# Top-32 attention and an ELU feed-forward block: sign bit into the shifted word, first scores by head, weights ahead of a pair of keys

## The chip, the cores and the metric

The kernel runs on one core of a Trainium2 chip. The metric is device time in microseconds (us) of one execution, the median over several runs. The engines are named as the profile names them: PE multiplies matrices (PEld is its loading of weights), DVE is the vector engine, ACT the scalar engine, POOL is GpSimd, and SP issues most of the transfers. Each engine works through its own list of instructions in order, and waits on semaphores for what other engines or transfers produce.

## The reference

The first block is attention that keeps, for each query, only the keys whose score is at least the 32nd largest. Its output, with the heads laid side by side, goes through a feed-forward block with an ELU between two products.

```python
# q, k, v: (8, 8, 576, 64) float32
scores = (1 / sqrt(64)) * q @ k.T
kth = np.partition(scores, -32, axis=-1)[..., -32:-31]
scores = np.where(scores >= kth, scores, -1e9)
scores = scores - max(scores)
attn = exp(scores); attn = attn / (sum(attn) + 1e-9)
x = (attn @ v) with heads side by side            # (4608, 512)
h = x @ w_in                                       # w_in (512, 2048), float64
g = where(h > 0, h, exp(min(h, 0)) - 1)
out = (g @ w_out).astype(float32)                  # w_out (2048, 512), float64
```

The two weight matrices arrive as float64. The kernel sees them as pairs of 32-bit words and turns them into float32 itself.

## The kernel before

**Steps.** The attention is cut into steps. A step is one tile of 128 queries of one batch and a pair of heads (for the last 64 queries of a batch, two pairs). There are four steps for a full tile and two for the remainder. `steps` holds all of them in order, and the main loop runs over `n`, where it searches step n, exponentiates step n-1, and multiplies step n-1 or n-2 by v. The first six steps (`EARLY = 6`) have their own branch of the loop, which computes the scores two steps ahead.

**The search (DVE).** For each of the two heads of a step, the 32 largest of 576 scores are found in four rounds: `first_max` (MAX8 at L373) and three times `next_max`, which replaces the eight found by a very low number (MATCH_REPLACE8 at L379) and searches again (MAX8 at L387). The eighth of the last round is the 32nd largest score.

**The mask.** In the first six steps `mask_early` makes three small numbers from that score (DVE L413, POOL L416, L417, L420 and L394), ACT applies a Relu with them as scale and bias (L428), and POOL subtracts the result from the scores (L431), once for each head. Later steps use `mask` on POOL alone (L399 to L401). ACT then exponentiates (L439).

**Start.** `load_qk(b, hp)` loads keys and queries of a pair of heads; for the first two pairs of batch 0 the queries go through ACT's queue, all else through SP's. `transpose_qk` turns them on PE into `kq` (L299, L307; copies L291, L292, L294). `scores(u, half)` makes, for one half of the keys, the products of both heads (L348) and copies them to `sc` with one copy (L368): 576 columns, 288 of each head. So a search of either head needs both halves. For the very first step the first half is copied by ACT and the second by DVE. `warm(n)` issues n transposes of the identity matrix on PE whose result nobody reads (L318). PSUM has two buffers (`ps_x`) that the transposes and the scores share.

**Decoding the weights.** The weights are 32 blocks of 128 by 512. `load_weights(most)` takes up to `most` entries of the list `loads` and issues them on SP's queue (L172); the first entry is three blocks, the second one, the third three. `weight_slot()` is called at set places between the search's rounds through `decode(n, place)`; each call joins the block that was split two calls earlier and splits the next one. Splitting is two passes on ACT: L182 writes a float32 from the high word, scaled, to the weight's place `dst`, and L183 scales the low word in place. Joining is on DVE and POOL: L188 shifts the words of `dst` left by three bits, L189 puts the sign bit of the high word into a word, and POOL's L193 adds the low word to the shifted one. The steps 0 to 3 have four decode places each, steps 4 and 5 five.

**Feed-forward.** When all heads of a tile are done, `sums` inverts the denominators on DVE (L451, L452), they go through DRAM and come back broadcast (`rb`), POOL scales the tokens (L547, `normalise`), and the pieces of the feed-forward block (`hidden` L567, `project` L591, with L581 to L584 for the ELU) become ready. `feed` issues such pieces on PE between the attention's products.

Of the kernel before, what the change touches and what calls it, by code (L numbers as in the profile page):

```python
# [10 lines left out]
FP32 = mybir.dt.float32  # L11
# [50 lines left out]
def kernel(  # L62
# [9 lines left out]
    nc = tc.nc  # L72
    P = nc.NUM_PARTITIONS
    B, H, S, D = q.shape
    dm, dff = moe_w_in.shape[0], moe_w_in.shape[1] // 2
    J = S // P
    JP = J * P
    R = S - JP
    HS = S // 2
# [17 lines left out]
    scpool = pool("sc", 5)  # L97
# [8 lines left out]
    ps_x = pool("ps_x", 2, space=PSUM)  # L106
# [78 lines left out]
    def join_weight(i):  # L185
        low, high, dst = words(i)
        bits = dst.bitcast(U32)
        nc.vector.tensor_scalar(bits, bits, 3, None, ALU.logical_shift_left)  # L188
        nc.vector.scalar_tensor_tensor(  # L189
            out=low, in0=high, scalar=0x80000000, in1=low,  # L190
            op0=ALU.bitwise_and, op1=ALU.bitwise_or,
        )
        nc.gpsimd.tensor_tensor(bits, bits, low, ALU.add)  # L193
        decoded[0] += 1
        del raw[i]
# [17 lines left out]
    def load_qk(b, hp):  # L213

        first = b == 0 and hp < 2
        aside = (b, hp) in ((0, 1), (0, 2))
        if aside:
            home = xtpool.tile([P, 2, NC * T // 2], FP32, tag="xT", name="kqin")
            home = home[:, :, 0 : (J + 1) * 2 * D].rearrange(
                "p n (j h d) -> p n j h d", j=J + 1, h=2  # L220
            )
        for n, (name, src) in enumerate((("k", k), ("q", q))):
            queue = nc.scalar if first and name == "q" else nc.sync
            if aside:
                t = home[:, n]
            else:
                t = ldpool.tile([P, J + 1, 2, D], FP32, tag="in", name=name + "in")
            queue.dma_start(
                t[:, 0:J, :, :],
                src[b, 2 * hp : 2 * hp + 2, 0:JP, :].rearrange(  # L230
                    "h (p j) d -> p j h d", j=J
                ),
            )
            queue.dma_start(
                t[0:R, J, :, :],
                src[b, 2 * hp : 2 * hp + 2, JP:S, :].rearrange("h p d -> p h d"),
            )
            loaded[b, hp, name] = t
# [75 lines left out]
    def warm(n):  # L314

        ps = ps_o.tile([P, dm], FP32, tag="o", name="idle")
        for _ in range(n):
            nc.tensor.transpose(ps[:, 0:P], ident[:], ident[:])  # L318
# [12 lines left out]
    def scores(u, half, copy=nc.scalar.copy):  # L331
# [35 lines left out]
                product(i, u.hps[0], i, slice(0, P), 0, ks)  # L367
        copy(u.sc[:, :, ks], ps[:, :, 0:HS])  # L368

    def first_max(u):  # L370
        u.m1 = small.tile([P, 2, 8], FP32, tag="m1", name="m1", bufs=2)
        for i in range(2):
            nc.vector.max(u.m1[:, i, :], u.sc[:, i, :])  # L373
        u.wk = wkpool.tile([P, 2, S], FP32, tag="wk", name="wk")
        u.m, u.cur = u.m1, u.sc
# [13 lines left out]
    def biases(u, early):  # L389
        u.neg = small.tile([P, 2], FP32, tag="neg", name="neg", bufs=2)  # L390
        if not early:
            u.nth = small.tile([P, 2], FP32, tag="nth", name="nth", bufs=2)
            nc.gpsimd.tensor_scalar_mul(u.nth[:], u.m[:, :, 7], -1.0)
        nc.gpsimd.tensor_scalar_mul(u.neg[:], u.m1[:, :, 0], -scale)  # L394
# [5 lines left out]
        nc.gpsimd.tensor_scalar(pen, pen, 0.0, TAKEN, ALU.min, ALU.max)  # L400
        nc.gpsimd.tensor_tensor(s, s, pen, ALU.add)  # L401

    def mask_early(u, between=None):

        kth = u.m[:, :, 7]
        field = small.tile([P, 2], U32, tag="field", name="field", bufs=2)
        minus = small.tile([P, 2], FP32, tag="minus", name="minus", bufs=2)
        neg = small.tile([P, 2], FP32, tag="nth", name="nth", bufs=2)  # L410
        pos = small.tile([P, 2], FP32, tag="pos", name="pos", bufs=2)
        one = 2.0**23
        nc.vector.tensor_scalar(  # L413
            field[:], kth.bitcast(U32), 0x7F800000, None, ALU.bitwise_and
        )
        nc.gpsimd.tensor_scalar(minus[:], field[:], 67 * one, -1.0, ALU.max, ALU.mult)  # L416
        nc.gpsimd.tensor_scalar_add(neg[:].bitcast(U32), minus[:], 560 * one)  # L417
        for i in range(2):
            at = slice(i, i + 1)
            nc.gpsimd.tensor_scalar(  # L420
                pos[:, at], kth[:, at], neg[:, at], -1.0, ALU.mult, ALU.mult
            )
        biases(u, True)
        if between is not None:
            between()
        for i in range(2):
            pen, s = u.wk[:, i, :], u.sc[:, i, :]
            nc.scalar.activation(  # L428
                pen, s, AF.Relu, scale=neg[:, i : i + 1], bias=pos[:, i : i + 1]
            )  # L430
            nc.gpsimd.tensor_tensor(s, s, pen, ALU.subtract)  # L431
# [112 lines left out]
    def normalise(g):  # L544
        blk = g.block
        x = blk.xT[:, :, g.cols]
        nc.gpsimd.tensor_tensor(x, x, g.rb[:, :, 0 : g.ql], ALU.mult)  # L547
        blk.left -= 1
        if blk.left == 0:
            ffn.extend(ffn_pieces(blk))  # L550
# [97 lines left out]
    steps, first, order = [], {}, []  # L648
    for b in range(B):
# [4 lines left out]
        for qt in (0, 1, 2, 3, 4) if b % 2 == 0 else (4, 0, 1, 2, 3):  # L654
            r0 = b * S + (JP if qt == J else qt)
            if qt == J:
                if b % 2 == 0:
                    half = blk, slot = places.pop(0)
# [29 lines left out]
    def decode(n, place):  # L688

        if place in ((2, 3, 4, 5, 6) if n in (4, 5) else (3, 4, 5, 6)):  # L690
            weight_slot()
# [39 lines left out]
    with tc.manual_schedule():  # L731
        load_qk(0, 0)
        nc.scalar.activation(rec[:], rec[:], AF.Copy)
        for hp in (1, 2):
            load_qk(0, hp)
        load_weights(3)
        warm(16)
        for hp in range(2):
            transpose_qk(0, hp, shared=hp == 0)
            steps[hp].kq = {hp: kqT[0, hp]}  # L740
            scores(steps[hp], 0)
            scores(steps[hp], 1, nc.vector.tensor_copy if hp == 0 else nc.scalar.copy)
            if hp == 0:
                load_qk(0, 3)
        load_weights()
        load_v(0, 0)
        first_max(steps[0])
# [4 lines left out]
        for n in range(NS + 4):  # L752
# [39 lines left out]
            if early:  # L792
                decode(n, 0)
                feed(n, 0.5)
                if last:
                    exp(last, 0)
                    exp(last, 1)
                next_max(now, (n, 1))
                decode(n, 2)
                if last:  # L800
                    trans(last)
                feed(n, 0.5)
                next_max(now, (n, 3), last)
                decode(n, 4)
                if last:
                    attend(last)
                if n in turns:
                    transpose_qk(*turns[n])
                if n < EARLY - 1:
                    warm(24)  # L810
                next_max(now, (n, 5))
                tile_ends = last and last.ends
                mask_early(now, (lambda: normalise(last.g)) if tile_ends else None)
                decode(n, 6)
                if n >= NHP - 2:
                    load_next()
                continue
# [63 lines left out]
```

## Time and profile before

| what | value |
|---|---|
| median of 3 runs | 1624.78 us (1624.5 to 1625.08) |
| profiled execution | 1623.01 us, its span 1621.2 us |
| mean granted PE clock | 0.991 of full |
| L387 MAX8 | 864, 748 ns each, 609.8 us in all |
| L379 MATCH_REPLACE8 | 576 and 288, 743 and 744 ns each |
| L182, L183 split passes on ACT | 32 each, median 0.68 us |
| L188 shift on DVE | 32, median 0.42 us, first at 16.7, last at 124.6 us |
| L189 sign bit on DVE | 32, median 0.68 us, longest 1.88 us |
| L193 add on POOL | 32, median 1.29 us |
| first three raw weight blocks | issued by SP at 8.21, landed 15.21 us |

The span runs from the first to the last instruction of the profiled execution. A line of a timeline gives the start in us, the length in us, the engine, the line of the kernel, the operation, what it writes and reads, and in square brackets how long the engine had stood idle and what ended that. One instruction's recorded length can overlap the next one's start by some hundredths, since the engine takes up the next while the last results are on their way out; so the distance of starts is the better measure of what an instruction costs its engine. The share of busy time is an average over the whole span, and says nothing of a single stage. The first 40th of the span is about 40 us.

```profile
PE   7878999999999999999999999999999999999999
...
DVE  7999999999999999999999999989999999899700
```

These two lines give the busy tenths of PE and DVE in 40 slices of the span.

### The profile page before, as it was taken

Reading aid. Unit: us, or ns where it says so; the run is one execution under the profiler, and the core shown is the slowest. Engines: PE = TensorE matmul, PEld = TensorE weight load, DVE = VectorE, ACT = ScalarE, POOL = GpSimd, SP = SyncE. Lnnn points to the kernel's source line nnn. Section 1 sums busy time; section 2 is a strip of 40 time slices with the busy share of each in tenths; the row PEclk is TensorE's granted clock in tenths of the full one; section 3 lists DMA queues with packets and bytes.
Section 4 is the critical chain, followed back from the end, with each engine's and each line's share of the span. In section 5 each row is a group of like instructions: output and inputs, shape, how many; then the busy total and the mean of one; then the engine's idle time right before and its main releaser. Section 6 shows DMA issues by size and latency. Waiting matters only on the chain.

```text
span 1621.2 us, 28833 instructions
## 1 busy us (share of the span) xinstructions
PE 1560.3 (96%) x9948; PEld 1066.8 (66%) x9948; DVE 1474.9 (91%) x3070; ACT 905.5 (56%) x1857; POOL 1141.6 (70%) x1448
## 2 busy tenths in 40 slices
PE   7878999999999999999999999999999999999999
PEld 5765778777675858676565665565565585757665
DVE  7999999999999999999999999989999999899700
ACT  6875666555564756565574575465475364545321
POOL 3777777777786878778687687678677676767621
PEclk8989999999999999999999999999999999999999
DMA  9773454442121413232423524333332552453300
GB/s 311 246 219 120 147 180 141 131 129 104 42 111 51 152 58 117 72 94 82 119 71 104 183 80 116 108 102 103 109 113 76 151 161 96 121 135 89 87 13 14
DMA packets 226706, 188.70 MB, mean 116 GB/s; under 512 B 180480, under 2 KB 188672, under 8 KB 226560
## 3 DMA queue, kind: packets, MB, share of 16 engines
q1 hardware_dynamic: 224192, 186.26, 38.1%
q8 instruction: 79, 1.29, 0.3%
q10 hardware_dynamic: 2368, 0.59, 0.2%
q14 instruction: 67, 0.55, 0.1%
HBM read 151.26 MB, written 35.54 MB: 115 GB/s over the span
## 4 chain that ended last, share of the span: by engine, by line
PE 80%; DVE 8%; POOL 5%; ACT 3%; issue 2%; DMA 1%; SPq 0%; DVEq 0%; POOLq 0%; ACTq 0%
PE ops L591 27%; PE hps L567 27%; PE avps L532 9%; PE scps L348 9%; PE eps L481 6%; DVE m L387 3%; DVE wk L379 3%; POOL sc L401 1%; POOL gT L584 1%; POOL wk L399 1%; POOL wk L400 1%; PE eps L499 1%; DVE raw L189 1%; PE qkps L299 0%; DVE m L373 0%
## 5 line engine op out<-in xcount | busy, mean ns | idle before, releaser
L387 DVE MAX8 m<-wk 128x8 f32<-128x576 f32 x864 | 609.8, 748 | 0.0
L567 PE MATMUL hps<-xT,w_in 128*128 128x256 f32 (+2 forms) x2560 | 531.8, 363 | 13.5 <-POOL xT L547 9.1
L591 PE MATMUL ops<-w_out,gT 128*128 128x512 f32 x1152 | 518.8, 596 | 7.5 <-ACT osb L600 7.5
L567 PEld LDWEIGHTS hps<-xT,w_in 128*128 128x128 f32 x2560 | 406.5, 193 | 118.8 <-issue 19.7
L379 DVE MATCH_REPLACE8 wk<-m,wk 128x576 f32<-128x576 f32 x576 | 423.6, 743 | 0.0
L401 POOL TENSOR_TENSOR sc<-sc,wk 128x576 f32<-128x576 f32 x276 | 389.4, 1411 | 23.1
L591 PEld LDWEIGHTS ops<-w_out,gT 128*128 128x128 f32 x1152 | 210.1, 190 | 244.4 <-issue 219.1
L439 ACT ACTIVATE sc<-sc,neg 128x576 f32<-128x576 f32 x288 | 224.1, 779 | 215.0 <-POOL sc L401 210.6
L584 POOL TENSOR_TENSOR gT<-gT,n 128x512 f32<-128x512 f32 (+1 forms) x160 | 186.4, 1169 | 178.7 <-ACT n L583 175.9
L368 ACT COPY sc<-scps 128x576 f32<-128x576 f32 x287 | 169.3, 641 | 118.3 <-PE scps L348 115.4
L399 POOL TENSOR_SCALAR wk<-sc,nth 128x576 f32<-128x576 f32 x276 | 207.1, 750 | 26.9
L379 DVE MATCH_REPLACE8 wk<-m,sc 128x576 f32<-128x576 f32 x288 | 211.8, 744 | 0.0
L373 DVE MAX8 m<-sc 128x8 f32<-128x576 f32 x288 | 201.0, 740 | 0.1
L348 PE MATMUL scps<-kq 64*128 64x288 f32 (+3 forms) x1344 | 181.5, 419 | 20.2 <-ACT sc L368 10.9
L400 POOL TENSOR_SCALAR wk<-wk 128x576 f32<-128x576 f32 x276 | 184.3, 668 | 22.9
L532 PE MATMUL avps<-et,vE 128*64 128x128 f32 (+1 forms) x3200 | 176.7, 266 | 6.0 <-ACT et L486 3.6
L532 PEld LDWEIGHTS avps<-et,vE 128*64 128x64 f32 x3200 | 158.9, 137 | 31.9 <-issue 23.7
L486 ACT COPY et<-eps 128x1024 f32<-128x1024 f32 x132 | 132.7, 1005 | 68.9 <-PE eps L481 67.6
L581 ACT ACTIVATE n<-hps 128x512 f32<-128x512 f32 (+1 forms) x160 | 88.9, 556 | 134.8 <-PE hps L567 132.0
L348 PEld LDWEIGHTS scps<-kq 64*128 64x128 f32 (+1 forms) x1344 | 101.9, 175 | 88.7 <-issue 32.6
L481 PEld LDWEIGHTS eps<-ident,sc 128*128 128x128 f32 x1056 | 122.1, 141 | 49.2 <-issue 31.9
L481 PE MATMUL eps<-ident,sc 128*128 128x128 f32 x1056 | 138.1, 273 | 6.4 <-ACT sc L439 3.4
(74 smaller groups left out, 957.4 us busy)
## 6 DMA issues: line engine op xcount, KB each, us to landing
kq<-kqd SPq DMA_DIRECT2D x152, 576.0 KB
kqd<-kq SPq DMA_DIRECT2D x32, 576.0 KB
rb<-recd SPq DMA_DIRECT2D x64, 128.0 KB
out_dram<-osb SPq DMA_DIRECT2D x32, 256.0 KB
ed<-sc SPq DMA_DIRECT2D x12, 576.0 KB
et<-ed SPq DMA_DIRECT2D x48, 144.0 KB
kin<-in_k_dram SPq DMA_DIRECT2D x18, 256.0 KB
qin<-in_q_dram SPq DMA_DIRECT2D x17, 256.0 KB
```

What stands on the lines that cost most here:

```text
L348: nc.tensor.matmul(ps[rows, j, at : at + keys.stop - keys.start], u.kq[hp][r, 1, q0 : q0 + g.ql], u.kq[hp][r, 0, keys], start=True, stop=True,
L373: nc.vector.max(u.m1[:, i, :], u.sc[:, i, :])
L379: nc.vector.match_replace(u.wk[:, i, :], u.m[:, i, :], u.cur[:, i, :], TAKEN)
L387: nc.vector.max(u.m[:, i, :], u.cur[:, i, :])
L399: nc.gpsimd.tensor_scalar(pen, s, u.nth[:, i : i + 1], 2.0**100, ALU.add, ALU.mult)
L401: nc.gpsimd.tensor_tensor(s, s, pen, ALU.add)
L439: nc.scalar.activation(s, s, AF.Exp, bias=u.neg[:, i : i + 1], scale=scale, accum_out=g.den[:, at : at + 1],)
L481: nc.tensor.transpose(ps[:, i, c * P : (c + 1) * P], e[:, k0 + c * P : k0 + (c + 1) * P], ident[:],)
L532: nc.tensor.matmul(g.av[r, hp, 0:ql], vE[g.b, hp][:, i, (c + i) % (J + 1), :], u.et[:, at, q0 : q0 + ql], start=(c == 0), stop=(c == J),)
L567: nc.tensor.matmul(ps[:, f % G, :], w_in[:, i, f * P : (f + 1) * P], blk.xT[:, i, 0:N], start=(i == 0), stop=(i == NC - 1),)
L584: nc.gpsimd.tensor_tensor(g, g, n, ALU.subtract)
L591: nc.tensor.matmul(blk.o[:], blk.gT[f // NG][:, f % NG, s * P : (s + 1) * P], w_out[:, f, :], start=(f == 0), stop=(f == NF - 1),)
```

## The change

Four things are changed. In `join_weight` the sign bit goes into the shifted word instead of the low word, so L189 reads the high word and `dst` and writes `dst`. The first step's scores are made by a new function, `scores_by_head`: both halves of one head, then a copy of that head, both copies on ACT; nine warming transposes stand ahead of them. The first entry of the list of weight loads is issued between the loads of the second and the third pair of heads. And in `mask_early` the step's last decode place is called before the Relu and the subtractions, where it stood after them.

```diff
@@ join_weight
         nc.vector.tensor_scalar(bits, bits, 3, None, ALU.logical_shift_left)
         nc.vector.scalar_tensor_tensor(
-            out=low, in0=high, scalar=0x80000000, in1=low,
+            out=bits, in0=high, scalar=0x80000000, in1=bits,
             op0=ALU.bitwise_and, op1=ALU.bitwise_or,
         )
         nc.gpsimd.tensor_tensor(bits, bits, low, ALU.add)
@@ new function
+    def scores_by_head(u):
+        u.sc = scpool.tile([P, 2, S], FP32, tag="sc", name="sc")
+        hp = u.hps[0]
+        for i in range(2):
+            ps = ps_x.tile([P, 2, JP], FP32, tag="x", name="scps")
+            r = slice(i * D, (i + 1) * D)
+            for half in range(2):
+                nc.tensor.matmul(
+                    ps[:, half, 0:HS],
+                    u.kq[hp][r, 1, u.g.qt * P : u.g.qt * P + u.g.ql],
+                    u.kq[hp][r, 0, half * HS : (half + 1) * HS],
+                    start=True,
+                    stop=True,
+                )
+            nc.scalar.copy(
+                u.sc[:, i, :].rearrange("p (n k) -> p n k", n=2), ps[:, :, 0:HS]
+            )
@@ mask_early
-    def mask_early(u, between=None):
+    def mask_early(u, n, between=None):
...
         biases(u, True)
+        decode(n, 6)
         if between is not None:
             between()
@@ start
-        for hp in (1, 2):
-            load_qk(0, hp)
-        load_weights(3)
+        load_qk(0, 1)
+        load_weights(1)
+        load_qk(0, 2)
+        load_weights(2)
         warm(16)
         for hp in range(2):
             transpose_qk(0, hp, shared=hp == 0)
             steps[hp].kq = {hp: kqT[0, hp]}
-            scores(steps[hp], 0)
-            scores(steps[hp], 1, nc.vector.tensor_copy if hp == 0 else nc.scalar.copy)
             if hp == 0:
+                warm(9)
+                scores_by_head(steps[0])
                 load_qk(0, 3)
+            else:
+                for half in range(2):
+                    scores(steps[hp], half)
@@ early steps
-                mask_early(now, (lambda: normalise(last.g)) if tile_ends else None)
-                decode(n, 6)
+                mask_early(
+                    now, n, (lambda: normalise(last.g)) if tile_ends else None
+                )
```

In the compiled kernel the order of instructions on PE differs only by the nine transposes. On DVE one copy is missing, on ACT and POOL the pairs of L182 and L183, and L193, stand before the Relus and the subtractions in the first six steps, and on SP the three raw weight blocks stand before the third pair.

## The prediction

> **What bounds the kernel now.** I read the page's busy table first, then busy time by stage, then the chain of waits around 150 us, because the change touches only the first 130 us and must reach the end through whatever sets the end.
>
> ```profile
> PE 1560.3 (96%) x9948; PEld 1066.8 (66%) x9948; DVE 1474.9 (91%) x3070; ACT 905.5 (56%) x1857; POOL 1141.6 (70%) x1448
> ...
> 37.90:83.00 45.10, 37.86 (x319) 32.59 (x318) 44.93 (x96) 36.01 (x65) 32.39 (x40) 0.92 0.79 243
> 83.00:130.00 47.00, 33.27 (x257) 27.14 (x258) 46.97 (x86) 35.53 (x66) 37.40 (x39) 0.89 0.61 191
> 130.00:158.00 28.00, 23.61 (x137) 13.97 (x135) 27.97 (x61) 15.28 (x31) 19.82 (x26) 1.00 0.38 109
> 158.00:1621.00 1463.00, 1439.21 (x9069) 971.92 (x9069) 1328.20 (x2774) 795.92 (x1655) 1038.37 (x1322) 1.00 0.35 105
> ```
>
> The stage rows give the window, its length, then PE, PEld, DVE, ACT and POOL busy. Up to 158 us it is DVE that never rests (46.97 of 47.00), and PE has gaps; from 158 us PE is full (1439 of 1463). So two bounds follow each other, and the hand-over decides what an early microsecond is worth:
>
> ```profile
> 148.12 0.74 DVE m L387
> 148.86 0.11 DVE rec L451
> ...
> 153.47 3.07 DMA rb<-recd
> ...
> 156.69 1.28 POOL xT L547
> ```
>
> DVE inverts the denominators at 148.8, their broadcast lands at 156.5, POOL scales the tokens, and PE's long run of hidden products starts at 158.02. What shifts DVE's inversion at 148.8 therefore shifts PE's full stretch, and with it the end, one for one. PE's 96% over the span hides that.
>
> The start in DVE's own order of time (start, length, what, idle before it):
>
> ```profile
> 10.28 0.76 DVE L368 COPY sc<-scps 128x576 f32<-128x576 f32 x1 [2.26 <-PE scps L348]
> 11.15 1.42 DVE L373 MAX8 m<-sc 128x8 f32<-128x576 f32 x2
> ...
> 16.71 0.42 DVE L188 TENSOR_SCALAR w_in<-w_in 128x512 uint32<-128x512 uint32 x1
> 17.04 0.68 DVE L189 SCALAR_TENSOR_TENSOR raw<-raw 128x512 uint32<-128x512 uint32 x1
> ...
> 22.13 0.43 DVE L188 TENSOR_SCALAR w_in<-w_in 128x512 uint32<-128x512 uint32 x1 [0.69 <-ACT w_in L182]
> 22.70 0.70 DVE L189 SCALAR_TENSOR_TENSOR raw<-raw 128x512 uint32<-128x512 uint32 x1
> 23.32 1.41 DVE L387 MAX8 m<-wk 128x8 f32<-128x576 f32 x2
> 24.76 0.17 DVE L413 TENSOR_SCALAR field<-m 128x2 uint32<-128x2 uint32 x1
> ```
>
> DVE starts its search at 11.15 and then stands still twice only, at 22.13 (0.69) and, alike, at 36.73 (0.60), both times for ACT's first half of a split weight. L189 there starts 0.57 after L188, where 0.33 is the undisturbed spacing, so it lost 0.24 more to ACT's second half.
>
> **The sums are differences on DVE's line up to 148.8**, minus is earlier. The profiled execution took 1623.01 around its span of 1621.2; the median is 1624.78, 1.8 above it, and the difference is put on the median.
>
> **(a) Scores head by head, with nine warming transposes.** PE's first scores ran 7.94 to 10.23, 2.29 for 8 records; the same 8 records took 1.24 at 12.92. The granted clock was 0.50 from 8.0 to 11.4 and 1.00 at 12.92, and PE had been busy only 1.86 of the 3.40 before 8.0. The nine transposes fill the gap from 6.80 to 7.94: 24 of them took 2.84 at full clock, so nine take 1.06 and are hidden by DVE's copy of the queries, which ends then anyway. If they run at the first sixteen's pace (3.32, so 1.87) they hold the scores back 0.7. With full clock, ACT's copy starts 0.80 after the scores (12.92 to 13.72), at 8.74, takes 0.64, and now covers a whole head: DVE's MAX8 on head 0 starts at 9.41. Head 1's copy ends 0.55 later, MAX8 needs it 0.66 later. DVE's own copy is gone, ACT has one more, where it idled 2.04 before. 11.15 to 9.41 is -1.74. With the low clock the copy waits 1.38 (7.94 to 9.32): -1.17; held back as well: -0.45. I take -1.74, since the gap before the scores closes.
>
> **(b) Raw weights before the third pair.** SP's load of three raw weights was issued at 8.21 and landed at 15.21, behind the third pair. Now it goes out after the second pair's keys, at about 4.1. The packets ahead of both end are the same, so the third pair lands no later than about 15.2, and the weights some 2.9 sooner (a pair is 590 KB, at 200 to 230 GB/s in this stretch), about 12.3. ACT is free for the first split at 13.5: its copies of the second step's scores end at 14.90 now, and move with the second pair's transposes, which wait for head 0's copy. Splits of two weights take 2.25 (15.23 to 17.48), so the third pair's copy starts at 15.74 instead of 17.48, and its eight transposes (1.09) fit before it. If the pair lands last of all, 0.3 is lost. In SP's queue the fourth pair's loads now stand behind the landing of the raw weights; PE reads that pair at 26.7, so nothing is late. ACT reaches the split for 22.13 1.74 to 2.7 sooner (by PE's clock at 17 us). DVE wants it 1.74 sooner, less two joins of (d): the stall of 0.69 shrinks to 0.47 or nothing, and the 0.24 goes. Together -0.70, from -0.93 to 0.
>
> **(c) The split ahead of the Relu in the first six steps.** ACT waited 1.37 for POOL's `pos` before the Relu at 26.35, and then did two split passes (1.1) before the next copies. They now fit in the wait, so the copies at 29.00 and everything after them on ACT come 1.1 sooner against DVE. PE's 48 warming transposes (6.13 after the third scores) and the fourth pair's transposes then limit it, still 2.75 sooner than before in all. The stall at 36.73 goes: 0.60 plus 0.23, -0.83 (to 0 if ACT is not sooner). On POOL the add L193 now precedes the two subtractions: it starts where POOL waited 0.57 for the Relu, pushes the subtractions 0.7 back, and lets the set end 0.5 sooner. The exponentials that wait for them (31.91, subtractions done at 30.09) cover that; without cover they would be 0.7 later, on ACT, not DVE.
>
> **(d) Sign bit into the shifted word.** L189 no longer reads ACT's second pass but what L188 has just written, and the compiled order has it wait for DVE's own semaphore. In 32 joins L188 (0.42) and L189 start 0.33 apart, overlapping by 0.09. No row shows this pair dependent. The nearest is L413 after the MAX8 it reads: MAX8 ends 24.73, L413 starts 24.76, where the independent L188 after MAX8 (17.64 plus 1.41, next start 18.97) starts 0.08 before the end. So 0.11 to 0.12 a join: 32 x 0.115 = +3.7. Below: 0, if the wait is free. Above: 0.12 x 32 = 3.8. L189's own 0.60 to the next start should not change. Queued behind it are the searches of all later steps, which is the critical line itself. I take +3.7.
>
> The Trainium skill speaks against this row: "VectorE: DVE Perf Modes", section "The DRAIN you can't avoid", says a semaphore after each of eight chained copies cost nothing (13.88 us both ways), because the next operation waits for the pipe anyway. By that rule (d) would be 0 and the whole sum -3.8. The trace shows starts ahead of the predecessor's end where there is no wait, so I go by the row.
>
> **(e) Collisions with POOL.** When POOL is inside a TENSOR_TENSOR, L188 and L189 finish only after it:
>
> ```profile
> 87.83 1.12 DVE L188 TENSOR_SCALAR w_out<-w_out 128x512 uint32<-128x512 uint32 x1
> 88.87 1.79 DVE L189 SCALAR_TENSOR_TENSOR w_out<-w_out 128x512 uint32<-128x512 uint32 x1
> ...
> 88.62 1.49 POOL L193 TENSOR_TENSOR w_out<-w_out,raw 128x512 uint32<-128x512 uint32 x1
> ```
>
> Five L189 took 1.8 instead of 0.68 (72, 89, 95, 115, 125 us), four L188 0.3 to 0.7 too long, 7.3 in all. At 72 the subtractions now end POOL's set at 72.7 (neg ends 68.63, add 1.3, two subtractions 2.8); L188 ends 0.28 after that, L189 at 73.69 instead of 73.98, although two joins of (d) lie before it: -0.5. The others hang on hundredths; I take them unchanged, with two collisions (2.2) more or less as bounds.
>
> **Sum:** -1.74 - 0.70 - 0.83 + 3.7 - 0.5 = -0.1. Forecast 1624.7, chance 0.58; its own range 1622.0 to 1627.3.
>
> **Rivals.**
> Rival A, the wait in (d) is free or mostly so: -3.8, 1621.0. For it: no row shows the pair itself. Against it: L413, and the transpose at 76.51, which starts 0.03 after the reciprocal it reads. Chance 0.20.
> Rival B, slower, POOL's set meets the joins more often: in steps 4 to 7 (69 to 127 us) POOL has up to seven TENSOR_TENSOR a step, and subtractions now end nearer to the next join. Each further hit costs 1.1. Two give 1626.9; from the third it is slower: 3.4 more than the forecast, 1628.1. For it: margins of 0.02 between L193's end and the next L188 (75.34, 75.36). Against: POOL's set ends sooner. Chance 0.14.
> Rival C, the change does not reach the end: PE's 2.84 idle before 158.02 is filled from elsewhere, and 1624.8 stays. For it: PE's 80% of the chain. Against: the hand-over above. Chance 0.08.
>
> **From these the numbers.** About 0.2% (3.25 us) is what a measurement of this kernel can tell from no change: 1621.5 and 1628.0. Faster 0.20 (A), slower 0.14 (B), within 0.66. The range 1620.6 to 1628.2 takes in A's and B's centres and leaves out about half of each, 0.17.
>
> **What would show it.** (a): first MAX8 near 9.4, granted clock 1.00 from 8.0 to 11.4. (b), (c): no idle before the third and seventh L188, weights landed near 12. (d): L188 and L189 0.45 apart instead of 0.33. (e): the count of L189 above 1.5 us, now five. The reciprocal at 148.8 and PE's run at 158.0 should both move by the change of the whole. I am wrong if the spacing in (d) stays at 0.33, if collisions number eight, or if the end moves by something that DVE's line at 148.8 does not show.

## The result, and the profile after

| kernel | median us | runs |
|---|---|---|
| before | 1624.62 (1621.77 to 1625.85) | 12 |
| after | 1628.71 (1626.73 to 1630.82) | 12 |

The ratio is 1.0026 (95% interval 1.0017 to 1.0035): 4.1 us slower (2.8 to 5.7), where 1624.7 was forecast. The profiled execution of after took 1630.68 us around a span of 1628.9, so it lies 2.0 above its median, and that of before 1.6 below the median of these twelve runs (1624.62). Of the 7.7 us between the two spans, 3.6 are the luck of two samples. Below, medians are compared with medians, and a profile is read for where things happen.

The busy time by stage in after (window, length, then PE, PEld, DVE, ACT, POOL busy, granted clock, DMA share, GB/s):

```profile
37.90:83.00 45.10, 37.34 (x305) 32.04 (x304) 43.45 (x91) 34.68 (x63) 30.11 (x38) 0.90 0.79 242
83.00:130.00 47.00, 34.85 (x259) 29.48 (x257) 46.51 (x82) 34.08 (x63) 35.05 (x38) 0.85 0.64 199
130.00:163.00 33.00, 28.58 (x149) 16.94 (x149) 32.93 (x69) 18.67 (x37) 22.78 (x28) 0.90 0.31 91
163.00:1628.00 1465.00, 1440.36 (x9069) 972.44 (x9069) 1328.29 (x2774) 795.90 (x1655) 1037.55 (x1323) 1.00 0.36 105
```

The picture is that of before: DVE without rest, then PE full. Only the border has moved, from 158 to 163, and DVE does fewer instructions in the same windows: from 83 to 130 us it gets through 82 where it did 86, although it is busy for all but 0.5 us. So it is slower while busy. DVE's rows of after (start, length, what, idle before it) show how:

```profile
10.25 1.42 DVE L392 MAX8 m<-sc 128x8 f32<-128x576 f32 x2 [1.86 <-ACT sc L385]
...
16.38 0.43 DVE L188 TENSOR_SCALAR w_in<-w_in 128x512 uint32<-128x512 uint32 x1 [0.49 <-ACT w_in L182]
...
21.89 0.43 DVE L188 TENSOR_SCALAR w_in<-w_in 128x512 uint32<-128x512 uint32 x1 [0.45 <-ACT w_in L182]
...
31.10 0.41 DVE L188 TENSOR_SCALAR w_in<-w_in 128x512 uint32<-128x512 uint32 x1
31.54 0.69 DVE L189 SCALAR_TENSOR_TENSOR w_in<-raw,w_in 128x512 uint32<-128x512 uint32 x1
...
51.53 0.43 DVE L188 TENSOR_SCALAR w_in<-w_in 128x512 uint32<-128x512 uint32 x1 [1.07 <-ACT w_in L182]
...
99.14 1.03 DVE L188 TENSOR_SCALAR w_out<-w_out 128x512 uint32<-128x512 uint32 x1
100.21 1.66 DVE L189 SCALAR_TENSOR_TENSOR w_out<-raw,w_out 128x512 uint32<-128x512 uint32 x1
...
103.23 1.05 DVE L432 TENSOR_SCALAR field<-m 128x2 uint32<-128x2 uint32 x1
...
153.90 0.17 DVE L471 RECIPROCAL rec<-den 128x8 f32<-128x8 f32 x1
```

L189 starts 0.44 after L188 (31.10 to 31.54), where before it was 0.33. In 26 joins of after that nothing else disturbs, the distance is 0.44 to 0.51. In all 32, held up or not, L189 starts 0.03 or 0.04 after L188 has ended, where in before it started 0.07 to 0.09 ahead of that end in 30 of 32 (the other two waited for ACT). L189's own length is unchanged (median 0.693 and 0.686). The search starts 0.90 earlier (10.25, before 11.15), and nothing of it is left at the reciprocal: 153.90, where it was 148.78. A MAX8 or MATCH_REPLACE8 is never longer than its kind. What is longer are L188, L189 and L432 (which is L413 of before), each while POOL is inside a TENSOR_TENSOR (one L189, at 126.80, inside a TENSOR_SCALAR). Such a lengthening is called a collision below. POOL's rows for the same time:

```profile
98.60 1.29 POOL L604 TENSOR_TENSOR gT<-gT,n 128x512 f32<-128x512 f32 x1 [4.49 <-ACT n L603]
99.85 1.47 POOL L193 TENSOR_TENSOR w_out<-w_out,raw 128x512 uint32<-128x512 uint32 x1
101.28 1.74 POOL L193 TENSOR_TENSOR w_out<-w_out 128x512 uint32<-128x512 uint32 x1
102.97 1.29 POOL L193 TENSOR_TENSOR w_out<-w_out,raw 128x512 uint32<-128x512 uint32 x1
```

POOL waits 4.49 for ACT, then runs four of them back to back, and DVE runs into three: L188 ends 0.28 after L604, L189 0.55 after the first L193 (DVE's 100.21 plus 1.66 is 101.87), and L432, a pass over two numbers a row, 0.02 after the last L193 has ended (104.26). PE's long run answers, 163.53 where it began at 158.02:

```profile
163.53 7.02 PE hps L587 x48
```

The reciprocal is 5.1 later, PE's run 5.5. So the border moved with DVE, as the prediction had it, and what has to be found is why DVE was not back at 148.8.

### The profile page after: what moved, and what is told of

It reads as the page before. It is cut to its first block, busy times and chain, and to the rows that moved or that the text cites. A ratio compares the mean times of both kernels' runs of the same rounds, so it can differ in the third digit from the quotient of the medians.

```text
span 1628.9 us, 28852 instructions
## 1 busy us (share of the span) xinstructions
PE 1569.3 (96%) x9957; PEld 1074.1 (66%) x9957; DVE 1478.5 (91%) x3069; ACT 907.5 (56%) x1858; POOL 1139.3 (70%) x1448
## 3 DMA queue, kind: packets, MB, share of 16 engines
q8 instruction: 79, 1.29, 0.3%
## 4 chain that ended last, share of the span: by engine, by line
PE 80%; DVE 7%; POOL 4%; DMA 3%; ACT 3%; issue 2%; SPq 1%; DVEq 0%; POOLq 0%; ACTq 0%
PE ops L611 28%; PE hps L587 26%; PE avps L552 9%; PE scps L348 9%; PE eps L501 6%; DVE wk L398 3%; DVE m L406 3%; POOL sc L420 1%; DMA vE<-in_v_dram 1%; POOL gT L604 1%; PE qkps L299 1%; POOL wk L418 1%; POOL wk L419 1%; PE eps L519 1%; DMA ed<-sc 1%
## 5 line engine op out<-in xcount | busy, mean ns | idle before, releaser
L604 POOL TENSOR_TENSOR gT<-gT,n 128x512 f32<-128x512 f32 (+1 forms) x160 | 186.3, 1169 | 183.3 <-ACT n L603 180.5
L348 PE MATMUL scps<-kq 64*128 64x288 f32 (+1 forms) x1336 | 179.8, 418 | 14.5 <-ACT sc L368 8.0
L506 ACT COPY et<-eps 128x1024 f32<-128x1024 f32 x132 | 132.7, 1005 | 71.8 <-PE eps L501 70.6
```

The source lines that it names most:

```text
L348: nc.tensor.matmul(ps[rows, j, at : at + keys.stop - keys.start], u.kq[hp][r, 1, q0 : q0 + g.ql], u.kq[hp][r, 0, keys], start=True, stop=True,
L604: nc.gpsimd.tensor_tensor(g, g, n, ALU.subtract)
```

## The experiments

Sixteen kernels, each timed in five rounds beside the kernel before on the same chip. The expectations stand as they were written ahead of each run. Theory 1 throughout is that the sign bit's part costs by a wait of DVE in each join, for what its own neighbour has just written; the others are put to the test one by one.

### The parts, apart and together

The sign bit alone (the first hunk of the change on the kernel before), and the change without it:

```diff
-            out=low, in0=high, scalar=0x80000000, in1=low,
+            out=bits, in0=high, scalar=0x80000000, in1=bits,
```

> The kernel before with the sign bit put into the shifted word, and nothing else of the change. Theory 1 (the loss is L189's wait for L188, 32 joins of 0.115 us on DVE's line): L188 to L189 are 0.45 apart, DVE's reciprocal moves from 148.8 to 151.5 to 153, and the kernel is 2.5 to 4.5 us slower than before. Rival 2 (the loss comes from the raw weights ahead of the third pair, which hold up the second pair's queries): within 1 us of before. Rival 3 (the loss comes from POOL's add ahead of the subtractions): within 1 us of before.

> The changed kernel with the sign bit put back into the low word; scores by head, load order and the early decode stay. Theory 1: 3 to 4.5 us faster than the changed kernel, so between 0.5 us faster and 1.5 us slower than the kernel before. Rivals 2 and 3: still 3 us or more slower than before.

The sign bit alone: 1628.67 against 1624.93, ratio 1.0023 (1.0014 to 1.0033). The change without it: 1624.37, 0.9998 (0.9989 to 1.0007). So the sign bit carries 3.7 of the 4.1 us, and the other three parts together are worth nothing that can be measured.

The change without the loads (the hunk "start" keeps `load_weights(3)` after both pairs), and the heads with the early decode place only:

```diff
-        load_qk(0, 1)
-        load_weights(1)
-        load_qk(0, 2)
-        load_weights(2)
+        for hp in (1, 2):
+            load_qk(0, hp)
+        load_weights(3)
```

> The changed kernel with the third pair loaded ahead of all raw weights again. Theory 1: the second pair's last queries are no longer late at 12.7 us, DVE is some 1 us earlier at 20 us, but the 32 waits stay: 1.5 to 4 us slower than before. Rival 2: no slower than before. Rival 3: 3 us or more slower than before.

> Scores by head with the warming transposes, and the early decode, without the sign bit and without the load order. Theory 1: DVE's start and its two stalls are gained and nothing is paid but collisions: 0.5 to 3 us faster than before. Rival 2: also no slower than before. Rival 3 (the add ahead of the subtractions costs): 2 us or more slower than before.

Without the loads 1628.63, 1.0025 (1.0014 to 1.0036), as slow as with them. Heads and decode place 1624.58, 1.0002 (0.9993 to 1.0011). Later the loads alone (the reverse of the diff above, on the kernel before) and the heads alone (`scores_by_head` and the nine transposes):

> The load order alone: the first raw weights ahead of the third pair, nothing else. Theory 8 (the raw weights' large packets hold up the second pair's last queries on ACT's queue): PE waits for those queries near 12 us, the first L182 starts later than the weights have landed, and the time is 0 to 2 us slower than before. If the order helps by itself, as the prediction had it: 0.3 to 1 us faster.

> Scores by head with the nine warming transposes alone. As the prediction had it: DVE's first MAX8 follows the copy L292 by 2.2 us instead of 3.95, and 1 to 1.7 us are gained at the end. Theory 9 (the copy of head 0 starts only when both heads' products are out, and the later stages take the gain back): 2.7 us behind L292, and within 0.7 us of before.

1623.36 against 1624.01, 0.9993 (0.9984 to 1.0001), and 1624.37, 0.9998 (0.9989 to 1.0007). Neither of these two moves the time by itself. The early decode place was not run alone, only together with the heads.

### Is it the wait? Four kernels without neighbours, and one with other neighbours

The sign bit goes into the shifted word, but the sign pass and the add of a block come one decode place after its shift (`join_weight` without L188, run for block i-3, and the shift for block i-2 behind it):

```diff
-        if i >= 2:
-            join_weight(i - 2)
+        if i >= 3:
+            join_weight(i - 3)
+        if 2 <= i < NW + 2:
+            shift_weight(i - 2)
```

> The kernel before with the sign bit put into the shifted word, as in the run with the sign alone, but the sign pass L194 (L189 of the other kernels) of a block comes one decode place after its shift L188, so that a pair of searches stands between them. Theory 1 (the wait for the instruction just ahead is the price): nothing waits, the sign pass's starts follow the instruction ahead without the 0.11 us, and the kernel is within 1.5 us of before, 2.5 us or more faster than with the sign alone. Rival 4 (the price is in the operands: reading and writing the weight's place instead of the low word): as slow as with the sign alone, 2.5 to 4.5 us over before. Rival 5 (POOL's add, which now waits for a later pass): slower than before by 1 to 3 us, with more L188 and sign passes over 1 us.

1629.4 against 1624.01, 1.0031 (1.0021 to 1.0041). That looks like the fall of Theory 1: no wait, and still slow. DVE's rows of this kernel (L194 is the sign pass here) say otherwise:

```profile
98.32 0.67 DVE L194 SCALAR_TENSOR_TENSOR w_out<-w_out 128x512 uint32<-128x512 uint32 x1
102.09 0.81 DVE L188 TENSOR_SCALAR w_out<-w_out 128x512 uint32<-128x512 uint32 x1 [3.10 <-ACT w_out L183]
...
104.26 0.17 DVE L420 TENSOR_SCALAR field<-m 128x2 uint32<-128x2 uint32 x1
```

The next instruction follows the sign pass and the shift after 0.59 or 0.60 and 0.33 or 0.34, the undisturbed distances. `field` of the fifth step comes 72.4 after the first search, where before had 71.6 and the sign bit alone 74.2: little is lost up to there. Then DVE stands for 3.10 us for a split, because ACT waits 2.93 for POOL's add, which now comes a place later. So the edit took the wait away and brought another. What the other destination itself costs can be told from a control with the same places, but the sign bit left in the low word (the diff is against the run above):

```diff
-            out=bits, in0=high, scalar=0x80000000, in1=bits,
+            out=low, in0=high, scalar=0x80000000, in1=low,
```

> Control for the run with the sign pass one decode place after the shift (1629.4 us): the same places, but the sign bit goes into the low word as in the kernel before, so nothing on DVE depends on its neighbour in either. Theory 1 (the sign bit costs only by the wait between neighbours): this control is as slow as that run, 1628.5 to 1630, ratio 1.003, since its loss came from the later place of POOL's add. Rival (the changed data path costs by itself, whatever stands between): this control is back at 1624 to 1625.5, ratio 1.000.

1629.92 against 1624.79, 1.0031 (1.0019 to 1.0043), the same ratio. The control has the same stall, to the hundredth, and another of 1.77 at 147 us (for POOL) where the run above has 0.53:

```profile
99.77 0.68 DVE L194 SCALAR_TENSOR_TENSOR w_out<-w_out 128x512 uint32<-128x512 uint32 x1
103.55 0.80 DVE L188 TENSOR_SCALAR w_out<-w_out 128x512 uint32<-128x512 uint32 x1 [3.10 <-ACT w_out L183]
```

A second pair puts the shift one search instruction ahead of its decode place and leaves the sign pass and POOL's add where they were, once with each destination (`shift_ahead` calls the shift of the next block; L188 goes from `join_weight`):

```diff
         for i in range(2):
             nc.vector.match_replace(u.wk[:, i, :], u.m[:, i, :], u.cur[:, i, :], TAKEN)
+            if between is not None and i == 0:
+                shift_ahead(*between)
...
         for i in range(2):
             nc.vector.max(u.m[:, i, :], u.cur[:, i, :])
+            if between is not None and i == 0:
+                shift_ahead(between[0], between[1] + 1)
```

> Kernel before with the sign bit put into the shifted word, but the shift issued one search instruction (0.66 us) ahead of its decode place, so that it and the sign pass are never neighbours, while the sign pass and POOL's add keep the places they have in the kernel before. Theory 1 (the loss is DVE's wait between two dependent neighbours): the loss is gone, 1624.8 us, ratio 1.000 (0.999 to 1.001); the sign pass starts 0.08 before the end of the search instruction ahead of it; reciprocal at 149.0 (148.3 to 150). Rival (the loss comes from the changed data path itself, that is from POOL's add now depending on a pass that writes the word it adds to, and from more collisions with POOL): it stays, 1628 to 1629, ratio 1.0022 to 1.003.

> Control for the run before: the same earlier place of the shift, but the sign bit goes into the low word as in the kernel before. Both theories: 1624.8 us (1624 to 1626), ratio 1.000. If it is slower, the earlier place itself costs (a collision of the shift with POOL or a wait for ACT), and the run before is to be read against this one: Theory 1 then wants the two equal within 0.1%, the rival 3 to 4 us apart.

1636.97 and 1637.21 against 1624.69: 1.008 (1.0067 to 1.0094) and 1.0077 (1.0065 to 1.009). Both are 12 us slower, which nobody expected, and they are equal, which Theory 1 did expect: with the passes apart, the two destinations are 0.2 us apart, where they were 3.7 apart with the passes side by side. Each ratio is known to about 0.0013, so the difference of the two only to about 3 us. The rows are sharper: in the first of the two the sign pass starts 0.07 to 0.10 ahead of the end of the instruction before it in all 32 joins, so none waits. The 12 us are told by two rows of the first of them, DVE's shift (L187 here) and POOL's add (L196):

```profile
32.71 1.32 DVE L187 TENSOR_SCALAR w_in<-w_in 128x512 uint32<-128x512 uint32 x1
33.95 0.08 DVE L382 MATCH_VALUE_LOAD wk<-m,wk 128x8 f32 x1
```

```profile
32.46 1.28 POOL L196 TENSOR_TENSOR w_in<-w_in,raw 128x512 uint32<-128x512 uint32 x1
```

The add starts at 32.46 and ends at 33.74, the shift starts inside it and ends at 34.03, 0.29 after it. Within a step the decode places are mostly 2.3 to 2.5 us apart, and an add fills 1.3 of that behind the sign pass; 0.66 earlier is inside the add of the block before. In the two kernels 26 and 27 shifts of 32 were longer than 0.6, in before 4. The excess over 0.42 sums to 17.7 and 17.1 us, in before to 2.0; the sign passes lost some 3 us less than in before.

Last, the wait without any weights: in the first six steps replace and search alternate, so that 36 MAX8 read what the instruction just ahead has written (in outline).

```diff
-            match_replace(head 0); match_replace(head 1); ...; max(head 0); max(head 1)
+            match_replace(head 0); max(head 0); ...; match_replace(head 1); max(head 1)
```

> Kernel before with no change to the weights; in the first six steps a search round runs replace, search of head 0 and then replace, search of head 1, where it ran both replaces and then both searches. 36 MAX8 then read what the neighbour just ahead has written (six steps, three rounds, two heads); nothing else is added. Theory 1: 0.11 to 0.12 each, +4.0 to +4.3 on DVE's line, reciprocal at 152.9, 1628.9 us (1627.9 to 1630), ratio 1.0025; replace and search start 0.77 to 0.78 apart, where two neighbours of the kernel before start 0.66 apart. By the rule that such a wait is free: 1624.8, ratio 1.000, spacing 0.66.

```profile
12.18 0.74 DVE L382 MATCH_REPLACE8 wk<-m,sc 128x576 f32<-128x576 f32 x1
12.95 0.76 DVE L385 MAX8 m<-wk 128x8 f32<-128x576 f32 x1
13.63 0.07 DVE L382 MATCH_VALUE_LOAD wk<-m,sc 128x8 f32 x1
```

From replace to the search that reads it 0.77, from that search to the next instruction, which doesn't read it, 0.68; two neighbours of before are 0.66 apart. 31 of the 37 such pairs in this stretch stand 0.77 to 0.79 apart. So 0.11 a wait is there on other operations, types and lines too, and 36 x 0.11 is 4.0. The time went up by less: 1626.35 against 1624.69, 1.0013 (1.0004 to 1.0022), so 0.6 to 3.6 us, below the 4.0 to 4.3 expected. The reciprocal came at 154.23 (148.78 in before), but PE's run at 162.25, 8.0 after it instead of 9.2. The price per wait is shown by the distances; how much of it reached the end here stays open.

### Where the three gains went

The trace of after has PE waiting for data in two places (start, length, what, idle before it):

```profile
12.76 0.29 PE L307 MATMUL qkps<-ident,kqin 64*128 64x64 f32 x1 [1.20 <-DMA kqin<-in_q_dram]
12.77 2.31 PE L348 MATMUL scps<-kq 64*128 64x288 f32 x8
...
20.52 6.98 PE L318 MATMUL idle<-ident 128*128 128x128 f32 x48
27.34 0.60 PE L299 MATMUL qkps<-ident,kin 128*128 128x128 f32 x4
...
37.59 2.92 PE L552 MATMUL avps<-et,vE 128*64 128x128 f32 x20 [3.11 <-DMA vE<-in_v_dram]
40.44 4.36 PE L318 MATMUL idle<-ident 128*128 128x128 f32 x24
44.73 1.24 PE L348 MATMUL scps<-kq 64*128 64x288 f32 x8
```

At 37.59 the first product with v waits for a load issued at 23.04 behind 4 MB of raw weights; then come warming transposes at a low clock, and the next scores at 44.73, where before had them at 43.38 (below). DVE pays at 51.53 (1.07, shown above).

```profile
30.04 1.24 PE L348 MATMUL scps<-kq 64*128 64x288 f32 x8 [2.01 <-ACT kq L294]
...
43.38 1.24 PE L348 MATMUL scps<-kq 64*128 64x288 f32 x8
```

So first, v ahead of the remaining raw weights, with heads and decode place:

```diff
-        load_weights()
-        load_v(0, 0)
+        load_v(0, 0)
+        load_weights()
```

> Scores by head, the early decode, and besides the first values (v of the first pair) loaded ahead of the two large weight loads instead of behind them; no sign bit, no load order. Theory 6 (what was gained at the start is lost again at the first product with v, which waits at 37.5 us for a load that stands behind 4 MB of weights): PE no longer waits there, the stalls of DVE after 36 us go, and the kernel is 0.5 to 2.5 us faster than scores by head and early decode alone. Rival 7 (the 48 warming transposes ahead of the fourth pair hold the start back, not v): PE waits for ACT at that product instead, and the time stays within 0.5 us of that kernel.

1624.16 against 1624.01, 1.0002 (0.9993 to 1.001): nothing, beside 1.0002 with v behind. The wait did go: PE starts that product at 36.47, 0.99 idle for ACT, where heads and decode place alone had 37.29 after 2.41 idle for v. But DVE stood 1.01 and 0.93 for ACT's splits at 22 and 37 us. Then the 48 warming transposes, which hold back the fourth pair: half of them left out, on the kernel before and on the change without the sign bit.

```diff
-                if n < EARLY - 1:
+                if 0 < n < EARLY - 1:
                     warm(24)
```

> Kernel before without the second 24 of the 48 warming transposes that PE runs between the third scores and the fourth pair's transposes (3.0 us). Control for the run after this one. The fourth pair's scores come up to 3.0 us sooner, but DVE in the kernel before waits nowhere for them: 1624.7, ratio 1.000 (0.999 to 1.001). If the missing transposes let PE's clock go down before the next products, 0 to 1 us slower.

> The change without the sign bit, and without those 24 warming transposes. Theory 7 (the 1.4 to 3 us that heads, loads and the early split win by the first steps are lost because the fourth pair's transposes stand behind the 48 warming transposes, so that the scores of step 4 come late and DVE waits 1.8 us near 51 us): the wait near 51 us goes, the reciprocal comes at 147.2 (146.5 to 148), 1622.8 us, ratio 0.9988 to 0.9992. Rival (the start is not what limits: what is won there is taken back by the first load of v, by ACT and by the collisions with POOL): no gain, 1624.5, ratio 0.9995 to 1.0005.

On the kernel before it is slower, 1627.5 against 1624.79, 1.0014 (1.0006 to 1.0023): the fourth pair's scores then take 2.29, at a granted clock of 0.50, instead of 1.24 at 1.00. They start at 31.32 where before had 30.04 (above), and DVE's second stall grows from 0.60 to 2.19:

```profile
31.32 2.29 PE L348 MATMUL scps<-kq 64*128 64x288 f32 x8 [4.15 <-ACT kq L294]
```

```profile
39.59 0.43 DVE L188 TENSOR_SCALAR w_in<-w_in 128x512 uint32<-128x512 uint32 x1 [2.19 <-ACT w_in L182]
```

With the three parts it is 1625.29, 1.0 (0.9991 to 1.0009), and there PE waits 5.51 for v and DVE 3.45 at 52.8. So leaving out the transposes alone does not keep the gain. At last the load of v and the second pair's queries are freed with all three parts in:

```diff
-        first = b == 0 and hp < 2
+        first = b == 0 and hp < 1
```

> The change without the sign bit, and the first load of v issued ahead of the remaining raw weights. Theory 8 (what heads, loads and the early split win by the first steps is lost near 51 us, where DVE waits 2.0 us for scores that PE could make only after a product with a v that landed at 37.4, behind 4 MB of raw weights): v lands near 25, PE waits for ACT there, the wait near 51 us goes and nothing takes its place; the reciprocal comes at 147.0 (146.3 to 147.8), 1622.5 us, ratio 0.9986 (0.998 to 0.9992). Rival (what is won at the start is not kept whatever frees that wait, since DVE then stands for ACT's splits or in collisions with POOL): ratio 0.9994 to 1.0006.

> As the run before, and the second pair's queries go through SP's queue like its keys, so that they are ahead of the first raw weights and no longer wait behind them (landed 7.1 us after their issue in the changed kernel). Theory 8: PE's idle time of 1.2 to 1.4 near 12.7 us goes, the splits start up to 0.5 sooner and DVE's first two waits for ACT (0.4 each) shrink; 1622.0 us, ratio 0.9984 (0.9978 to 0.999). Rival: ratio 0.9994 to 1.0006, as for the run before.

1623.74 against 1624.08, 0.9994 (0.9985 to 1.0002), and with the queries too (the diff above) 1624.94, 0.9997 (0.9988 to 1.0005). In the first of them PE no longer waits for v, and the scores come 5.3 us earlier than in after:

```profile
35.32 1.38 PE L552 MATMUL avps<-et,vE 128*64 128x128 f32 x20 [0.99 <-ACT et L506]
...
39.40 1.24 PE L348 MATMUL scps<-kq 64*128 64x288 f32 x8
```

```profile
16.25 0.43 DVE L188 TENSOR_SCALAR w_in<-w_in 128x512 uint32<-128x512 uint32 x1 [0.65 <-ACT w_in L182]
...
21.96 0.43 DVE L188 TENSOR_SCALAR w_in<-w_in 128x512 uint32<-128x512 uint32 x1 [0.74 <-ACT w_in L182]
...
99.51 1.05 DVE L432 TENSOR_SCALAR field<-m 128x2 uint32<-128x2 uint32 x1
100.48 0.41 DVE L188 TENSOR_SCALAR w_out<-w_out 128x512 uint32<-128x512 uint32 x1
100.81 1.78 DVE L189 SCALAR_TENSOR_TENSOR w_out<-w_out 128x512 uint32<-128x512 uint32 x1
```

The wait near 51 us is gone, as expected, but the time did not fall as expected. This is what each profile shows on DVE's line between its first search and the reciprocal (stalls: idle times above 0.15 us, after 12 us; collisions: L188 above 0.42, L189 above 0.69, `field` above 0.17, summed):

| kernel | first MAX8 | reciprocal | stalls | collisions |
|---|---|---|---|---|
| before | 11.15 | 148.78 | 1.29 | 7.58 |
| sign bit alone | 10.32 | 152.73 | 1.58 | 8.46 |
| after | 10.25 | 153.90 | 2.01 | 8.97 |
| without the sign bit | 10.06 | 148.99 | 2.82 | 7.19 |
| loads alone | 10.39 | 149.71 | 1.41 | 8.80 |
| heads alone | 10.93 | 149.84 | 2.02 | 8.11 |
| three parts, v first | 9.96 | 149.27 | 1.70 | 8.78 |

Read by rows: a start up to 1.2 earlier is spent on stalls and collisions, in another mixture each time. Without the sign bit the line is 1.30 longer (138.93 against 137.63), of which 1.53 more stall and 0.39 less collision make 1.14. With v first it is 1.68 longer: 0.41 and 1.20 make 1.61. For the sign bit alone it is 4.78 longer: 0.29 and 0.88, and 32 waits of 0.115, 3.7, make 4.9. For after it is 6.02: 0.72, 1.39 and 3.7 make 5.8.

The same columns settle Theory 1. Take stalls and collisions from the line: 128.8 to 129.1 us are left in the five kernels of the table without the sign bit in the shifted word, 132.4 and 132.7 in the two with it. The four kernels with the passes apart leave 128.5 and 128.8 (one place apart) and 128.7 and 128.8 (shift ahead), whichever word the sign bit goes into. So with the passes apart the destination costs nothing, and side by side it costs 3.6 to 3.9, the size of 32 waits.

No kernel here beats before beyond its interval; the loads alone come nearest.

## Why the prediction was wrong

**What held.** (d), the wait in each join, was right in its place, its kind and its size: distances of mostly 0.44 to 0.46 instead of 0.33, +3.7 predicted, +3.7 measured for the sign bit alone (2.3 to 5.4). It is the neighbourhood that costs, as two pairs of controls show. Rival A, the free wait, fell. The Trainium skill, "VectorE: DVE Perf Modes", section "The DRAIN you can't avoid", reports that a semaphore after each of eight chained copies cost nothing. No run here has such copies; for the pairs of this case the measurement decides otherwise, 0.44 against 0.33 for the shift and sign pass and 0.77 against 0.66 for the search. The hand-over held too: the reciprocal moved by 5.1 and PE's run by 5.5. Rival C fell.

**The step that failed is the other side of the sum:** (a) -1.74, (b) -0.70 and (c) -0.83, -3.27 together, measured with all three in (the change without the sign bit) as -0.3 (-1.8 to +1.1), which can't be told from nothing. The first search did come earlier, but in the profiles new stalls and collisions behind it took it back, and the sum had no term for the first and held the second as good as unchanged.

- (a) was mis-sized, and by its row. DVE's copy of the queries to the first MAX8 took 3.95 in the one profile that the step was read from (7.20 to 11.15), with a granted clock of 0.74 from 6.5 to 9.5 (first rows below). In the eight other kernels whose first scores were left as before it took 2.90 or 2.91 seven times, at a clock of 1.00, and 3.76 once, at 0.82. With the heads it took 2.68 to 2.74 in all nine kernels, at 1.00. So the edit usually wins 0.2, and 1.2 where the clock happens to be low; the working took the rare case for the rule. The clock did go to 1.00 as predicted, and the nine transposes took 1.20. The copy of head 0 started 1.28 after the scores (8.30 to 9.58), not 0.80: 0.80 was read where one copy follows one half of both heads. Here it follows both halves of one head, and all eight records took 1.36. Record by record, the copy of one half in before (13.72) started when the fourth of eight had ended (13.67), the copy of head 0 here (9.58) when the seventh had (9.54). So the heads' products were interleaved, and the first head was done hardly earlier than the second; what interleaves them was not tried. Below are DVE's row and the window's row of before, then the unwarmed start in the kernel with the loads alone, at full clock.

```profile
7.20 0.82 DVE L292 COPY kq<-qkps 128x512 f32<-128x512 f32 x2 [6.31 <-ACT kq L291]
```

```profile
6.50:9.50 3.00, 1.86 (x9) 1.35 (x10) 0.82 (x2) 0.88 (x3) 0.00 (x0) 0.74 1.37 213
```

```profile
7.49 0.82 DVE L292 COPY kq<-qkps 128x512 f32<-128x512 f32 x2 [6.61 <-ACT kq L291]
9.53 0.76 DVE L368 COPY sc<-scps 128x576 f32<-128x576 f32 x1 [1.21 <-PE scps L348]
10.39 1.42 DVE L373 MAX8 m<-sc 128x8 f32<-128x576 f32 x2
```

```profile
6.50:9.50 3.00, 1.84 (x14) 0.98 (x11) 0.82 (x2) 1.16 (x3) 0.00 (x0) 1.00 1.15 325
```

- (b) missed the queue beside it. The weights' packets were through at 12.1, near the forecast, well before ACT got to the first split at 15.68. It was ACT that was late: the second pair's last queries, 32 KB issued on ACT's queue at 5.60, landed at 12.7, after 7.1 us beside the raw weights on SP's queue. The last packets on ACT's queue ended at 12.0 to 12.1 in all five kernels with the new load order and these queries on that queue, and at 8.9 to 9.4 in all twelve with the old order. The second step's scores waited for the queries (PE's 1.20 above) and then ran at a granted clock of 0.54, 2.31 for eight records. The stall of 0.69 at 22 us shrank to 0.45, and one of 0.49 at 16.38 is new. The step had argued that the packets ahead of both ends were the same, and did not count those on ACT's queue.
- (c) took the wait before the Relu (it is 0.2 to 0.3 now), and the stall near 37 us went. DVE then pays later, at 51 us: PE waits for the first v, the scores come late, and DVE stands for 1.07.
- (e) was -0.5 and came out as +1.4 in this profile. `field` is a victim that the working had not listed: in every profile with the early decode place it lost 0.88 or more in one step or two, and in none of the others that leave the shift in its place. The costly hit (0.9) is the same in all eight of these profiles: near 100 us it meets the second or third of three adds L193 that queue behind POOL's L604, which had waited 3.4 to 4.5 for ACT; in before it waited 1.40. That the early decode place makes ACT late there was not tested.

Rival B had the time (1628.1) by the wrong road: one more microsecond of collisions, not three hits. With (a) to (c) at nothing and the rest as predicted the sum is +3.2, and +4.1 was measured.

**Open.** That stalls and collisions take back whatever the start wins is shown row by row for single profiles. That they must is not: the collisions range from 7.2 to 9.0 in the seven kernels of the table, which is more than the 1.2 us at stake, and no kernel removed them.

## What to carry to other kernels

On an engine that sets the end, two dependent instructions should not be neighbours: here each such pair cost 0.11 us, and the remedy must leave the other engines' places alone, since moving the shift 0.66 us cost more (12 us) than the wait did (3.7). A gain read from a single profile's start is to be checked against the clock granted there, above all if the clock is what the gain comes from. A microsecond won early is only won if the next wait behind it, for data, for another engine or for a shared resource, has been priced too.

## What the runs showed of the hardware

- A dependent neighbour on DVE starts 0.11 us later than an independent one, for uint32 passes (0.44 against 0.33) and for the float32 search (0.77 against 0.66).
- DVE's TENSOR_SCALAR and SCALAR_TENSOR_TENSOR on words in SBUF seldom end inside a TENSOR_TENSOR of POOL that they start in. Of 213 that would have at their usual length (18 profiles, up to 170 us) 197 ended after it: a shift by 0.28 or 0.29, a sign pass by 0.55 to 0.57, a `field` by 0.03. The other 16 started within 0.41 of POOL's start, and there POOL's took longer, 1.7 to 2.2 instead of 1.3 or 1.4. A shift of 0.42 took 1.32 and ended 0.29 after it, and a pass over two numbers a row took 1.05 instead of 0.17. MAX8 and MATCH_REPLACE8 beside the same POOL instructions kept their 0.7 us. The Trainium skill, "SBUF — State Buffer", section "SBUF: two separate sides", explains the like by a pair of ports that whichever of the two engines starts first holds for a whole instruction. These figures agree with it in kind; the runs don't show the ports.
- Small transfers on ACT's queue beside large ones on SP's landed late: 32 KB of queries in 7.1 us, their last packet ending at 12.1 together with the last of the 1.5 MB of weights issued 1.3 earlier. Without the weights beside them, in before, their last packet ended at 8.9, 3.5 after issue.
- 24 warming transposes that nobody reads were worth 2.3 us (1.0 to 3.7): without them the next scores took 2.29 at a granted clock of 0.50, with them 1.24 at 1.00.
